# A decode step of gated attention plus a gated feed-forward on one core: the rows of Wd split unevenly over the partitions, and 31 weight rows multiplied 512 columns at a time

## The chip, the cores and the metric

One Trainium2 chip, one core of it. The metric is device time in microseconds (us) of one launch. Three runs of the kernel before gave 196.21, 196.41 and 196.93 us, a median of 196.41 us. The profile shown below is of one further execution.

## The reference

```
x = A_x                                          # 4 x 1 x 512, bf16
g = sigmoid((x * gate_w).sum(-1))
# a: attention over the last 4096 of 16384 cached positions
q = (x @ wq)                                     # 32 heads of 128; wq 512 x 4096
k, v = k_cache[:, :, -4096:], v_cache[:, :, -4096:]   # 4 batches, 8 kv heads, each used by 4 q heads
p = softmax(q k^T * 128 ** -0.5)
a = (p v) @ wo                                   # wo 4096 x 512
# b: gated feed-forward
gate, up = x @ W_gate, x @ W_up                  # 512 x 1792 each
h = gate * (gate > 0) * up
b = h @ W_down                                   # 1792 x 512
out = g * a + (1 - g) * b                        # 4 x 1 x 512
```

All inputs are bf16. The data is about 81 MB, nearly all of it the windows of the two caches, and every byte is used once for four query rows.

## The kernel before

**Stages.** The 32 pairs of batch and kv head are worked in NSET = 8 sets of four. For each set the K window (4 MB) is loaded to Ksb, transposed on TensorE by `kt` (16 fills of a PSUM bank, copied back by ACT L371 and DVE L373), multiplied with q in `scores` (L387), reduced to a maximum, exponentiated (L424), transposed on DVE (L431) and multiplied with V in `values` (L442). `combine` (L456 to L466) sums the partial results of a set and writes its scaled columns into `oq`. Ksb and Vsb hold two sets each, so the load of set s waits for the last use of set s-2.

**The end.** After the last K set, `gateup` (L468) multiplies x with W_gate and W_up and DVE makes `hT` (L477 to L487). Then TensorE runs `values` of set 7, `combine(7)`, and `product` (L542): the sum over Wd rows and wo rows that makes the output. Wd here is 1792 rows laid out as 14 rows on each of 128 partitions (`Vsb`, slot 0). wo is 32 rows on each of 128 partitions (`Wbig`). One row i is one product of a 128 x 4 stationary operand with a 128 x 512 moving operand. `product` does it as four matmuls of 128 columns, `cb` = 0 to 3, each to its own 32-partition group of bank AB, so that the four groups of the array work at once. At the end DVE and ACT copy the four quarters to `outr` (L561, L563), two engines for each half u, and SP stores it (L587).

**Queues.** All large loads are issued by SP, in this order at the end: W_gate, W_up, V of set 7, Wd (waits for `values` of set 6, ("PV", 6, 3)), then wo in pieces by WO_CUTS: rows 0 to 16, 16 to 26, 26 to 30, and rows 30 to 32 as two loads of 256 columns each ("WOL", 0 and 1). Each load has a semaphore of its own that counts to 16, one for each of the 16 DMA engines that carry it. The wo loads wait for nothing but ("Q",), far earlier; they queue behind what was issued ahead of them.

**Order on the engines.** Every engine runs its own list in the order in which `P.op` was called. PE's list near the end is: `combine(6)`, `gateup`, `values(7)`, `combine(7)`, 14 rows of Wd, then the wo rows, each group behind the wait for its load. DVE's list near the end is the four operations of `gateup`, the copy L448, three operations of `combine(7)` (L461 to L464), and the final copies.

Of the kernel before, what the change touches and what calls it, by code (L numbers as in the profile page):

```python
# [5 lines left out]
FP32 = mybir.dt.float32  # L6
BF16 = mybir.dt.bfloat16
ACTF = mybir.ActivationFunctionType
ALU = mybir.AluOpType
# [8 lines left out]
WIN = 4096  # L18
FF = 1792
NSET = 8  # L20
NFT = FF // 128
FQ = FF // 4
SCALE = DH ** -0.5
NEG = -1.0e9
LOWEST = -3.0e38
# [1 line left out]
NTR = 4  # L27
NSC = 2
NPIECE = 2
NBANK = 4  # L30
NFILL = 16
WO_CUTS = (0, 16, 26, 30)
ACT_TAKES = (0, 1, 4, 6, 8, 9, 11, 13, 14)
LOOP_FIRST = 2
LOOP_TURNS = 3
# [107 lines left out]
def bass_gated_mix__sliding_block_cached__glu_gated_reglu__decode_kernel(  # L143
# [13 lines left out]
    with ExitStack() as ctx:  # L157
        def sb(name, shape, dt):
            return ctx.enter_context(nc.sbuf_tensor(name, shape, dt))

        Ksb = sb("Ksb", [128, 2, 16384], BF16)
        Vsb = sb("Vsb", [128, 2, 16384], BF16)
# [12 lines left out]
        S32 = sb("S32", [128, 32], FP32)  # L175
        xsb = sb("xsb", [5, 512], BF16)
        xT = sb("xT", [128, 4, 32], BF16)
# [14 lines left out]
        ssum = sb("ssum", [128, 2], FP32)  # L192
        recip = sb("recip", [128, 2], FP32)
        oq = sb("oq", [128, 128], BF16)
        hrelu = sb("hrelu", [128, FQ], FP32)
        hrow = sb("hrow", [128, FQ], FP32)
        hcol = sb("hcol", [128, FQ], FP32)
        hT = sb("hT", [128, NFT * 4], BF16)
        outr = sb("outr", [4, 512], BF16)
        banks = [ctx.enter_context(nc.psum_tensor("bank%d" % i, [128, 512], FP32)) for i in range(8)]  # L200
        TR = banks[0:NTR]
        SCB = banks[NTR:NTR + NSC]
# [5 lines left out]
        Wu = Ksb[:, 0, 4 * FF:8 * FF].rearrange("p (t f) -> p t f", t=4)  # L208
        Wd = Vsb[:, 0, 0:NFT * 512].rearrange("p (i w) -> p i w", w=512)
        Wq3 = Wbig[:, :].rearrange("p (t w) -> p t w", t=4)  # L210
        Wo3 = Wbig[:, :].rearrange("p (i w) -> p i w", w=512)

        P = Program()
# [14 lines left out]
        def load_v(s):  # L228
            P.dma("sp", lambda e: e.dma_start(Vsb[:, s % 2, :], heads(A_v_cache, s)), ("V", s),
                  [("PV", s - 2, 3)] if s >= 2 else [], sem=loop_sem("V", s))  # L230
# [4 lines left out]
        for s in range(1, NSET):  # L235
# [4 lines left out]
        P.dma("sp", lambda e: e.dma_start(Ksb[:, 0, 4 * FF:8 * FF], B_W_up.rearrange("(p t) f -> p (t f)", p=128)),  # L240
              ("WU",), [("SC", NSET - 2, NBANK - 1)])
        load_v(NSET - 1)
        P.dma("sp", lambda e: e.dma_start(Vsb[:, 0, 0:NFT * 512], B_W_down.rearrange("(p i) w -> p (i w)", p=128)),
              ("WD",), [("PV", NSET - 2, 3)])
        wo_src = A_wo.rearrange("(p i) w -> p (i w)", p=128)
        for k in range(len(WO_CUTS) - 1):
            lo, hi = 512 * WO_CUTS[k], 512 * WO_CUTS[k + 1]
            P.dma("sp", lambda e, lo=lo, hi=hi: e.dma_start(Wbig[:, lo:hi], wo_src[:, lo:hi]), ("WO", k), [("Q",)])  # L248
        wo_src3 = A_wo.rearrange("(p i) w -> p i w", p=128)
        for u in range(2):  # L250
            P.dma("sp", lambda e, u=u: e.dma_start(Wo3[:, WO_CUTS[-1]:32, 256 * u:256 * u + 256],
                                                   wo_src3[:, WO_CUTS[-1]:32, 256 * u:256 * u + 256]), ("WOL", u), [("Q",)])


        P.op("pool", lambda e: e.memset(ones[:, :], 1.0), ("ONES",))
# [6 lines left out]
        for a in range(4):  # L262
            r = slice(32 * a, 32 * a + 32)
# [20 lines left out]
        P.op("dve", lambda e: e.memset(xw[:, :], 0.0), ("XW0",))  # L284
        P.op("dve", lambda e: e.memset(xT[:, :, :].rearrange("p t r -> p (t r)"), 0.0))
        P.op("dve", lambda e: e.memset(mcol[:, :], 0.0))
        P.op("dve", lambda e: e.memset(mrow2[:, :], 0.0), ("M0",))
        P.op("dve", lambda e: e.memset(qW[:, :, :, :].rearrange("p s h w -> p (s h w)"), 0.0), ("QZ",))

# [14 lines left out]
        for t in range(4):  # L304
            P.op("pe", lambda e, t=t: e.matmul(FB[:, 32:36], gwB[:, t * 128:(t + 1) * 128], xT[:, t, 0:4],
                                               start=(t == 0), stop=(t == 3)),
# [5 lines left out]
        for half in range(2):  # L312
            for t in range(4):
                for g in range(4):
# [3 lines left out]
                        start=(t == 0), stop=(t == 3), tile_position=(0, 32 * g)),  # L318
                        ("Q",) if (half == 1 and t == 3 and g == 3) else ("QH",) if (half == 0 and t == 3 and g == 3) else None,
                        [("WQ",), ("XTC",)])  # L320
        for half in range(2):
            src = SCB[half][:, :].rearrange("p (h w o) -> p h o w", h=4, o=2)
            for cc in range(2):
                dst = qrow[:, half, :].rearrange("p (h o c w) -> p h o c w", h=4, o=2, c=2)[:, :, :, cc, :]
                which = [("Q",) if half else ("QH",)]
# [6 lines left out]
        for half in range(2):  # L332
            for hh in range(4):
                for o in range(2):
                    base = 32 * half + 16 * o + hh
                    lo = 256 * hh + 128 * o
# [17 lines left out]
        def copy_done(f):  # L354
            return ("KTC",) + fills[f]
# [110 lines left out]
                 ("OQ", s), [("RECIP", s), ("G",)], sem="vd")  # L466

        def gateup():  # L468
            for which, W, key in ((0, Wg, "WG"), (1, Wu, "WU")):
                for t in range(4):  # L470
                    for g in range(4):
                        P.op("pe", lambda e, which=which, W=W, t=t, g=g: e.matmul(
                            TR[which][32 * g:32 * g + 32, 0:FQ], xT[:, t, :], W[:, t, FQ * g:FQ * g + FQ],
                            start=(t == 0), stop=(t == 3), tile_position=(0, 32 * g)),
                            ("GU", which) if (t == 3 and g == 3) else None,
                            [(key,)] + [copy_done(f) for f in range(NSET * NFILL - NTR, NSET * NFILL)])
            P.op("dve", lambda e: e.tensor_scalar(hrelu[:, :], TR[0][:, 0:FQ], 0.0, None, op0=ALU.max),  # L477
                 ("H0",), [("GU", 0)])
            P.op("dve", lambda e: e.tensor_tensor(
                hrow[:, :].rearrange("p (i c) -> p c i", i=NFT), TR[1][:, 0:FQ].rearrange("p (c i) -> p c i", i=NFT),  # L480
                hrelu[:, :].rearrange("p (c i) -> p c i", i=NFT), ALU.mult), ("H1",), [("H0",), ("GU", 1)])
            P.op("dve", lambda e: e.transpose(hcol[:, :], hrow[:, :]), ("H2",), [("H1",)])
            P.op("dve", lambda e: e.tensor_tensor(
                hT[:, :].rearrange("p (i b) -> p i b", b=4),
                hcol[:, :].rearrange("p (i b) -> p i b", b=32)[:, :, 0:4],
                gsb[:, 4:8].rearrange("p (o b) -> p o b", o=1).to_broadcast([128, NFT, 4]), ALU.mult),
                ("H",), [("H2",), ("G",)], sem="vd")  # L487
# [43 lines left out]
        for k in range(NPIECE):  # L531
            exponent(NSET - 1, k)
            turn(NSET - 1, k)
        combine(NSET - 2)
        gateup()
        for k in range(4):
            values(NSET - 1, k)
        combine(NSET - 1)
        AB = SCB[0]
        oq3 = oq[:, :].rearrange("p (b i) -> p b i", b=4)  # L540

        def product(stat, mov, cb, start, stop, name, waits):  # L542
            P.op("pe", lambda e: e.matmul(AB[32 * cb:32 * cb + 4, 0:128], stat, mov[:, 128 * cb:128 * cb + 128],  # L543
                                          start=start, stop=stop, tile_position=(0, 32 * cb)), name, waits)

        for i in range(NFT):
            for cb in range(4):
                product(hT[:, 4 * i:4 * i + 4], Wd[:, i, :], cb, i == 0, False, None,
                        [("WD",), ("H",), ("SCC", NSET - 1, NBANK - 1)])
        for k in range(len(WO_CUTS) - 1):  # L550
            for i in range(WO_CUTS[k], WO_CUTS[k + 1]):
                for cb in range(4):
                    product(oq3[:, :, i], Wo3[:, i, :], cb, False, False, None, [("WO", k), ("OQ", NSET - 1)])
        for u in range(2):
            for i in range(WO_CUTS[-1], 32):
                for cb in (2 * u, 2 * u + 1):
                    product(oq3[:, :, i], Wo3[:, i, :], cb, False, i == 31,
                            ("ACC", u) if (i == 31 and cb == 2 * u + 1) else None, [("WOL", u)])
        for u in range(2):
            for cb, eng in ((2 * u, "dve"), (2 * u + 1, "act")):  # L560
                fn = (lambda e, cb=cb: e.tensor_copy(outr[:, 128 * cb:128 * cb + 128], AB[32 * cb:32 * cb + 4, 0:128])) \  # L561
# [71 lines left out]
```

## Time and profile before

| what | value |
|---|---|
| runs | 196.21, 196.41, 196.93 us |
| the profiled execution | 196.08 us |
| its span | 194.8 us |
| HBM read | 81.01 MB, 416 GB/s over the span |
| PE busy | 135.3 us (69%) |
| DVE busy | 105.2 us (54%) |
| ACT busy | 63.8 us (33%) |
| Wd load, from issue to landing | 16.9 us |
| mean granted TensorE clock | 0.86 |

The page cuts the span into 40 slices of 4.87 us. A digit is the busy share of an engine in that slice in tenths; 9 means 90% or more. DMA is the mean busy share of the core's 16 DMA engines and GB/s what they moved. PEclk is the TensorE clock that was granted, in tenths of full speed. The chain of waits follows the last instruction back to what released it, step by step. In tables by stretch, the columns are the stretch and its length, then for each engine busy us and number of instructions, then the granted clock, the DMA share and GB/s.

The profiled execution's own time is 1.28 us over its span; what lies around the span is not seen in the trace.

### The profile page before, as it was taken

Reading aid. Unit: us, or ns where it says so; the run is one execution under the profiler, and the core shown is the slowest. Engines: PE = TensorE matmul, PEld = TensorE weight load, DVE = VectorE, ACT = ScalarE, POOL = GpSimd, SP = SyncE. Lnnn points to the kernel's source line nnn. Section 1 sums busy time; section 2 is a strip of 40 time slices with the busy share of each in tenths; the row PEclk is TensorE's granted clock in tenths of the full one; section 3 lists DMA queues with packets and bytes.
Section 4 is the critical chain, followed back from the end, with each engine's and each line's share of the span. In section 5 each row is a group of like instructions: output and inputs, shape, how many; then the busy total and the mean of one; then the engine's idle time right before and its main releaser. Section 6 shows DMA issues by size and latency. Waiting matters only on the chain.

```text
span 194.8 us, 3947 instructions
## 1 busy us (share of the span) xinstructions
PE 135.3 (69%) x1696; PEld 103.3 (53%) x1696; DVE 105.2 (54%) x282; ACT 63.8 (33%) x112; POOL 7.3 (4%) x37
## 2 busy tenths in 40 slices
PE   0135399779299929991999199929993999723834
PEld 0112387556197618860885097619762886402623
DVE  1104056896548654955594548554866595690201
ACT  2002135673055307430752065306530742310001
POOL 7300000000000000000000000000000000000000
PEclk9999669999759997999699759985999699785885
DMA  6999999999999999999999999999999999999993
GB/s 223 437 431 431 431 444 427 437 426 447 437 431 441 424 434 431 432 427 424 431 431 431 431 431 426 431 431 431 431 437 431 431 406 433 446 437 402 416 409 103
DMA packets 3885, 81.17 MB, mean 417 GB/s; under 512 B 409, under 2 KB 930, under 8 KB 1058
## 3 DMA queue, kind: packets, MB, share of 16 engines
q1 hardware_dynamic: 3864, 81.01, 97.3%
q8 instruction: 8, 0.13, 0.3%
q14 instruction: 3, 0.02, 0.0%
q10 hardware_dynamic: 10, 0.01, 0.0%
HBM read 81.01 MB, written 0.00 MB: 416 GB/s over the span
## 4 chain that ended last, share of the span: by engine, by line
DMA 60%; PE 32%; DVE 6%; issue 1%; ACT 1%; SPq 1%; DVEq 0%
DMA Ksb<-in_A_k_cache_dram 47%; PE bank L366 21%; DMA Wbig<-in_A_wo_dram 12%; PE bank L387 5%; DVE Ksb L373 3%; PE bank L442 2%; PE bank L456 2%; PE bank L543 1%; DVE sc L395 1%; DVE pT L431 1%; ACT Ksb L371 1%; DVE mq L402 0%; DVE negmax L416 0%; SPq L248 0%; SPq L581 0%
## 5 line engine op out<-in xcount | busy, mean ns | idle before, releaser
L366 PE MATMUL bank<-identw,Ksb 128*128 128x128 f32 x512 | 78.7, 316 | 26.8 <-DMA Ksb<-in_A_k_cache_dram 26.8
L366 PEld LDWEIGHTS bank<-identw,Ksb 128*128 128x128 f32 x512 | 69.5, 165 | 36.4 <-DMA Ksb<-in_A_k_cache_dram 28.6
L371 ACT COPY Ksb<-bank 128x512 f32<-128x512 f32 x72 | 41.1, 586 | 87.4 <-PE bank L366 87.3
L373 DVE COPY Ksb<-bank 128x512 f32<-128x512 f32 x56 | 37.6, 685 | 43.5 <-PE bank L366 43.4
L395 DVE CUSTOM_DVE_ANT_0 sc<-bank,mask 128x512 bf16<-128x512 f32 x32 | 21.7, 679 | 7.5 <-PE bank L387 7.3
L442 PE MATMUL bank<-Vsb,pT 128*32 128x256 bf16 x512 | 20.5, 287 | 6.9 <-DMA Vsb<-in_A_v_cache_dram 6.9
L387 PE MATMUL bank<-Ksb,qS 128*32 128x512 bf16 x256 | 20.1, 389 | 4.6 <-DVE Ksb L373 4.1
L431 DVE STREAM_TRANSPOSE pT<-sc 128x1024 bf16<-128x1024 bf16 x16 | 19.7, 1236 | 1.4 <-ACT sc L424 1.3
L442 PEld LDWEIGHTS bank<-Vsb,pT 128*32 128x32 bf16 x512 | 13.1, 100 | 13.4 <-issue 9.7
L424 ACT ACTIVATE sc<-sc,negmax 128x1024 bf16<-128x1024 bf16 x16 | 18.4, 1150 | 5.3 <-DVE negmax L416 5.2
L456 PEld LDWEIGHTS bank<-osb,Wsel 128*64 128x64 f32 x128 | 8.5, 144 | 5.3 <-issue 2.8
L456 PE MATMUL bank<-osb,Wsel 128*64 128x32 f32 x128 | 9.4, 229 | 2.0 <-DVE osb L448 2.0
L387 PEld LDWEIGHTS bank<-Ksb,qS 128*32 128x32 bf16 x256 | 4.2, 94 | 11.8 <-DVE Ksb L373 6.7
L563 ACT CAST outr<-bank 4x128 bf16<-4x128 f32 x2 | 0.5, 258 | 21.9 <-PE bank L543 21.8
L448 DVE COPY osb<-bank 128x256 f32<-128x256 f32 x8 | 3.4, 420 | 6.6 <-PE bank L442 6.6
L543 PE MATMUL bank<-Wbig,oq 128*4 128x128 bf16 x128 | 3.8, 286 | 4.2 <-DMA Wbig<-in_A_wo_dram 4.2
L298 PE MATMUL bank<-identw,xw 5*128 5x5 f32 x4 | 0.6, 263 | 8.6 <-DVE xw L292 8.6
L348 POOL COPY qS<-qW 128x64 bf16<-128x64 bf16 x8 | 1.8, 237 | 118.7 <-PE bank L387 106.4
L543 PEld LDWEIGHTS bank<-Wbig,oq 128*4 128x4 bf16 x128 | 2.8, 109 | 5.2 <-DMA Wbig<-in_A_wo_dram 5.2
L316 PE MATMUL bank<-Wbig,xT 128*32 128x512 bf16 x32 | 3.6, 631 | 2.6 <-DMA Wbig<-in_A_wq_dram 2.6
L561 DVE CAST outr<-bank 4x128 bf16<-4x128 f32 x2 | 0.6, 282 | 8.6 <-PE bank L543 8.6
L416 DVE TENSOR_SCALAR negmax<-mall 32x1 f32<-32x1 f32 x32 | 4.6, 144 | 1.0
(58 smaller groups left out, 51.2 us busy)
## 6 DMA issues: line engine op xcount, KB each, us to landing
Ksb<-in_A_k_cache_dram SPq DMA_DIRECT2D x8, 4096.0 KB, 23.4
Vsb<-in_A_v_cache_dram SPq DMA_DIRECT2D x8, 4096.0 KB, 32.5
Wbig<-in_A_wq_dram SPq DMA_DIRECT2D x1, 4096.0 KB, 12.1
Wbig<-in_A_wo_dram SPq DMA_DIRECT2D x1, 2048.0 KB, 21.4
Ksb<-in_B_W_gate_dram SPq DMA_DIRECT2D x1, 1792.0 KB, 17.5
Ksb<-in_B_W_up_dram SPq DMA_DIRECT2D x1, 1792.0 KB, 21.4
Vsb<-in_B_W_down_dram SPq DMA_DIRECT2D x1, 1792.0 KB, 16.9
Wbig<-in_A_wo_dram SPq DMA_DIRECT2D x1, 1280.0 KB, 24.0
```

What stands on the lines that cost most here:

```text
L316: P.op("pe", lambda e, half=half, t=t, g=g, col=col: e.matmul(SCB[half][32 * g:32 * g + 32, 0:512], xT[:, t, :], Wq3[:, t, col:col + 512], ...
L366: P.op("pe", lambda e, bk=bk, cc=cc, c=c, s=s: e.transpose(bk[:, cc * 128:(cc + 1) * 128], Kw[:, s % 2, c * 128:(c + 1) * 128], identw[:, :]),
L371: P.op("act", lambda e: e.copy(dst, bk[:, :]), ("KTC", s, i), [("KT", s, i)], sem="va")
L373: P.op("dve", lambda e: e.tensor_copy(dst, bk[:, :]), ("KTC", s, i), [("KT", s, i)], sem="vd")
L387: P.op("pe", lambda e, a=a, o=o: e.matmul(bk[32 * a:32 * a + 32, 0:512], qS[:, s % 2, o, :], k4[:, 16 * bank:16 * bank + 16, 32 * a:32 * a ...
L395: P.op("dve", lambda e: e.tensor_tensor_reduce(sc[:, s % 2, bank * 512:(bank + 1) * 512], bk[:, :], mask[:, :], 1.0, LOWEST, ALU.add, ALU.max,
L416: P.op("dve", lambda e, a=a: e.tensor_scalar(negmax[32 * a:32 * a + 32, par:par + 1], mall[:, 0:1], -SCALE, None, op0=ALU.mult), ("NEGMAX" ...
L424: P.op("act", lambda e: e.activation(sc[:, par, k * PW:(k + 1) * PW], sc[:, par, k * PW:(k + 1) * PW], ACTF.Exp, bias=negmax[:, par:par + ...
L431: P.op("dve", lambda e: e.transpose(pT[:, par, k * PW:(k + 1) * PW], sc[:, par, k * PW:(k + 1) * PW]), ("PTT", s, k), [("EXP", s, k), ("PV ...
L442: P.op("pe", lambda e, c=c, g=g, blk=blk: e.matmul(OB[32 * g:32 * g + 32, 0:256], pT[:, par, 32 * blk:32 * blk + 32], Vsb[:, par, 256 * bl ...
L456: P.op("pe", lambda e, k=k, lo=lo: e.matmul(FB[r, 384:416], Wsel[:, lo:lo + 64], osb[:, par, 32 * k:32 * k + 32], start=(k == 0), stop=(k ...
L543: P.op("pe", lambda e: e.matmul(AB[32 * cb:32 * cb + 4, 0:128], stat, mov[:, 128 * cb:128 * cb + 128], start=start, stop=stop, tile_positi ...
```

## The change

Three things are changed.

Wd's layout: 1792 rows are no longer 14 on each partition. The first 1408 are 11 on each of 128 partitions (NFA), and the other 384 are 6 more on each of partitions 0 to 63 (NFB). The 384 rows are brought by eight loads of eight partitions each (32q+k, 32q+k+4, ..., 32q+k+28), 6 KB a partition. `gateup` follows the layout: columns of W_gate and W_up that belong to the 384 rows go to two further PSUM banks, and DVE works the two parts one after the other; `hrow` has a part that is set to zero at the start.

The products: 11 + 6 Wd rows and the first 14 wo rows (NBULK) are each one matmul of 512 columns; row n goes to partition group n % 4 of bank DB. DB is zeroed by DVE first. When all 31 are done, DVE copies DB to `bulk`, and four fp32 matmuls with a 0/1 matrix (S32) add the four groups into AB. The other 18 wo rows go on as before.

The wo loads: WO_CUTS is (0, 14, 24, 30) in place of (0, 16, 26, 30), and rows 30 to 32 come in one load.

```diff
-NFT = FF // 128
-FQ = FF // 4
+NFA = 11
+NFB = 6
+NFT = NFA + NFB
+FQ = 32 * NFA
+FB0 = 128 * NFA
+FE = 32 * NFB
-WO_CUTS = (0, 16, 26, 30)
+WO_CUTS = (0, 14, 24, 30)
+NBULK = 14
...
-        P.dma("sp", lambda e: e.dma_start(Vsb[:, 0, 0:NFT * 512], B_W_down.rearrange("(p i) w -> p (i w)", p=128)),
+        P.dma("sp", lambda e: e.dma_start(Vsb[:, 0, 0:NFA * 512],
+                                          B_W_down[0:FB0, :].rearrange("(p i) w -> p (i w)", p=128)),
               ("WD",), [("PV", NSET - 2, 3)])
+        wd_src = B_W_down[FB0:FF, :].rearrange("(q h k i) w -> q k h (i w)", q=2, h=8, i=NFB)
+        for q in range(2):
+            for k in range(4):
+                P.dma("sp", lambda e, q=q, k=k: e.dma_start(
+                    Vsb[32 * q + k:32 * q + 32:4, 0, NFA * 512:NFT * 512], wd_src[q, k]),
+                    ("WE", q, k), [("PV", NSET - 2, 3)])
...
-        for u in range(2):
-            P.dma("sp", lambda e, u=u: e.dma_start(Wo3[:, WO_CUTS[-1]:32, 256 * u:256 * u + 256],
-                                                   wo_src3[:, WO_CUTS[-1]:32, 256 * u:256 * u + 256]), ("WOL", u), [("Q",)])
+        P.dma("sp", lambda e: e.dma_start(Wo3[:, WO_CUTS[-1]:32, :], wo_src3[:, WO_CUTS[-1]:32, :]), ("WOL",), [("Q",)])
...
+        P.op("dve", lambda e: e.memset(hrow[64:128, 32 * NFA:32 * NFT], 0.0), ("HZ",))
...
+                for t in range(4):
+                    for g in range(2):
+                        P.op("pe", lambda e, which=which, W=W, t=t, g=g: e.matmul(
+                            TR[2 + which][32 * g:32 * g + 32, 0:FE], xT[:, t, :], W[:, t, FB0 + FE * g:FB0 + FE * g + FE],
+                            start=(t == 0), stop=(t == 3), tile_position=(0, 32 * g)),
+                            ("GU", which) if (t == 3 and g == 1) else None, [(key,)] + last)
...
-        for i in range(NFT):
-            for cb in range(4):
-                product(hT[:, 4 * i:4 * i + 4], Wd[:, i, :], cb, i == 0, False, None,
-                        [("WD",), ("H",), ("SCC", NSET - 1, NBANK - 1)])
-        for k in range(len(WO_CUTS) - 1):
+        DB = SCB[1]
+        P.op("dve", lambda e: e.memset(DB[:, :], 0.0), ("DB0",), [("SCC", NSET - 1, NBANK - 1)], sem="vd")
+        rows = [(hT[:, 4 * i:4 * i + 4], Wd[:, i, :], [("WD",), ("H",)]) for i in range(NFA)]
+        rows += [(hT[0:64, 4 * i:4 * i + 4], Wd[0:64, i, :], [("WE", q, k) for q in range(2) for k in range(4)]) for i in range(NFA, NFT)]
+        rows += [(oq3[:, :, i], Wo3[:, i, :], [("WO", 0), ("OQ", NSET - 1)]) for i in range(NBULK)]
+        for n, (stat, mov, waits) in enumerate(rows):
+            g = n % 4
+            P.op("pe", lambda e, g=g, n=n, stat=stat, mov=mov: e.matmul(
+                DB[32 * g:32 * g + 4, 0:512], stat, mov, start=(n < 4), stop=(n >= len(rows) - 4),
+                tile_position=(0, 32 * g)), ("BULK",) if n == len(rows) - 1 else None, waits + [("DB0",)])
+        P.op("dve", lambda e: e.tensor_copy(bulk[:, :], DB[:, :]), ("BULKC",), [("BULK",)], sem="vd")
+        for cb in range(4):
+            product(S32[:, 0:4], bulk, cb, True, False, None, [("BULKC",), ("SCC", NSET - 1, NBANK - 2), ("WSUM",)])
+        for k in range(1, len(WO_CUTS) - 1):
             for i in range(WO_CUTS[k], WO_CUTS[k + 1]):
...
-                            ("ACC", u) if (i == 31 and cb == 2 * u + 1) else None, [("WOL", u)])
+                            ("ACC", u) if (i == 31 and cb == 2 * u + 1) else None, [("WOL",)])
```

More of the change, by code (lines that the diff above doesn't have):

```diff
@@ L194, in bass_gated_mix__sliding_block_cached__glu_gated_reglu__decode_kernel @@
         oq = sb("oq", [128, 128], BF16)
-        hrelu = sb("hrelu", [128, FQ], FP32)
-        hrow = sb("hrow", [128, FQ], FP32)
-        hcol = sb("hcol", [128, FQ], FP32)
+        hrelu = sb("hrelu", [128, 32 * NFT], FP32)
+        hrow = sb("hrow", [128, 32 * NFT], FP32)
+        hcol = sb("hcol", [128, 32 * NFT], FP32)
         hT = sb("hT", [128, NFT * 4], BF16)
         outr = sb("outr", [4, 512], BF16)
+        bulk = sb("bulk", [128, 512], FP32)
         banks = [ctx.enter_context(nc.psum_tensor("bank%d" % i, [128, 512], FP32)) for i in range(8)]
@@ L468, in gateup @@
         def gateup():
+            last = [copy_done(f) for f in range(NSET * NFILL - NTR, NSET * NFILL)]
             for which, W, key in ((0, Wg, "WG"), (1, Wu, "WU")):
@@ L474, in gateup @@
                             start=(t == 0), stop=(t == 3), tile_position=(0, 32 * g)),
[L475 to L481, printed above, removed]
+                            None,
+                            [(key,)] + last)
+                for t in range(4):
[4 more added lines that the diff above has]
+                            ("GU", which) if (t == 3 and g == 1) else None, [(key,)] + last)
+            parts = ((slice(0, 128), 0, 0, NFA), (slice(0, 64), 2, NFA, NFT))
+            for k, (r, bk, lo, hi) in enumerate(parts):
+                P.op("dve", lambda e, r=r, bk=bk, lo=lo, hi=hi: e.tensor_scalar(
+                    hrelu[r, 32 * lo:32 * hi], TR[bk][r, 0:32 * (hi - lo)], 0.0, None, op0=ALU.max),
+                    ("H0", k), [("GU", 0)])
+            for k, (r, bk, lo, hi) in enumerate(parts):
+                P.op("dve", lambda e, r=r, bk=bk, lo=lo, hi=hi: e.tensor_tensor(
+                    hrow[r, 32 * lo:32 * hi].rearrange("p (i c) -> p c i", c=32),
+                    TR[bk + 1][r, 0:32 * (hi - lo)].rearrange("p (c i) -> p c i", c=32),
+                    hrelu[r, 32 * lo:32 * hi].rearrange("p (c i) -> p c i", c=32), ALU.mult),
+                    ("H1",) if k else None, [("H0", k), ("GU", 1), ("HZ",)])
             P.op("dve", lambda e: e.transpose(hcol[:, :], hrow[:, :]), ("H2",), [("H1",)])
```

## The prediction

> **What bounds the kernel now.** I read the page's slices first.
>
> ```profile
> DMA  6999999999999999999999999999999999999993
> GB/s 223 437 431 431 431 444 427 437 426 447 437 431 441 424 434 431 432 427 424 431 431 431 431 431 426 431 431 431 431 437 431 431 406 433 446 437 402 416 409 103
> ...
> q8 instruction: 8, 0.13, 0.3%
> q14 instruction: 3, 0.02, 0.0%
> ```
>
> The DMA engines are full from the second slice to the last but one, at about 431 GB/s, 26.9 GB/s for each of 16. Nothing but the order, the amount and the spread of bytes moves the time, except in the last slice. There the chain of waits shows what ends last:
>
> ```profile
> 165.91 0.33 SPq L243
> ...
> 166.28 0.43 SPq L248
> ...
> 166.75 24.00 DMA Wbig<-in_A_wo_dram
> ...
> 190.80 1.24 PE bank L543 x30
> ...
> 192.05 0.83 PE bank L543 x20
> ...
> 192.90 0.28 DVE outr L561
> ```
>
> wo's second piece lands at 190.75; from there PE has work to 193.14, then copies and the store. Two things end close together, PE's last 64 matmuls and the last loads, as the timeline shows:
>
> ```profile
> 190.80 2.34 PE L543 MATMUL bank<-Wbig,oq 128*4 128x128 bf16 x64 [1.60 <-DMA Wbig<-in_A_wo_dram]
> 192.05 0.52 PEld L543 LDWEIGHTS bank<-Wbig,oq 128*4 128x4 bf16 x20 [0.30 <-DMA Wbig<-in_A_wo_dram]
> 192.75 0.10 PEld L543 LDWEIGHTS bank<-Wbig,oq 128*4 128x4 bf16 x4 [0.18 <-DMA Wbig<-in_A_wo_dram]
> ```
>
> The last load is in at about 192.71, and 0.43 us later PE is done. The stretches show how the loads run out:
>
> ```profile
> 188.00:190.00 2.00, 1.20 (x56) 0.91 (x44) 0.00 (x0) 0.00 (x0) 0.00 (x0) 0.54 0.98 387
> 190.00:191.00 1.00, 0.20 (x12) 0.20 (x16) 0.00 (x0) 0.00 (x0) 0.00 (x0) 0.50 0.75 274
> 191.00:191.90 0.90, 0.90 (x40) 0.75 (x30) 0.00 (x0) 0.00 (x0) 0.00 (x0) 0.50 0.53 179
> 191.90:192.40 0.50, 0.49 (x24) 0.31 (x16) 0.00 (x0) 0.00 (x0) 0.00 (x0) 0.50 0.30 88
> ```
>
> The share does not fall at once: for 0.9 us it stands at 0.53, half of the engines. The trace's semaphore increments, sixteen a load, say the same: for the last load seven arrive at 190.78 to 191.15, one at 191.64, eight at 192.48 to 192.71. **Eight engines are 1.6 us late.** The first K load's sixteen lay within 0.5 us (22.12 to 22.61), so the lag was gathered on the way. From load to load single increments jump back, after the packets of q8 and q14. The page prices them: 0.3% of 16 engines x 194.8 us is 9.4 us for 8 q8 packets, 1.2 us each; with the data packet behind it each costs its engine 1.5 us. Followed by phase, the seven q8 packets ahead of the end strike seven different engines; of the three q14 packets two strike one further engine (about 1.0 us each, so 2.0 us late and the last of all), one strikes the engine that is at 191.64.
>
> **Part 1, Wd's spread.** Each engine carries the rows of eight partitions. If the engines of partitions 0 to 63 are eight and the others eight, 14 KB x 8 = 112 KB of Wd each become 17 KB x 8 = 136 KB on one half and 88 KB on the other: 24 KB at 26.9 GB/s is 0.91 us more on the one and 0.91 us less on the other. By the packets (14336 bytes 0.54 us, 10240 bytes 0.385, 4096 bytes 0.159) the sums are 8 x 0.54 = 4.3 before, 8 x 0.42 + 8 x 0.24 = 5.3 after: 1.0 us. I take +1.0 and -0.9. Whether that helps hangs on which engines are late. The trace names none, so both bounds stay: all late ones in the half relieved, or some not.
>
> What speaks for a clean split: the count of eight; and the engines that took the small loads of x and gate_w (partitions 0 to 4) at the start, so far as they can be followed, stay early. What speaks against it: q8 strikes seven engines and q14 two that are none of these. If q8's eight packets have one half of the engines to themselves, as no engine is struck twice, then the engine that q14 struck twice lies in the other half, the one that gets 24 KB more. I hold this the likelier.
>
> [...]
>
> Their issues: SP takes 0.43 us each (L248), 8 x 0.43 = 3.5 us, so wo's first issue goes from 166.28 to about 169.8. It lands at 187.65, 18 us behind; V of set 7 and Wd are still queued, and nothing starves. Nothing else but the store waits on SP. Cover gone, it would cost 3.5 us.
>
> **Part 2, the gate and up products.** 16 more matmuls on PE and 4 more DVE operations (L477 to L482 took 2.2 us; with two parts about 3). PE then waits 6.9 us for V of set 7, DVE 6.56 us. Nothing, and up to 1 us if V came early, which it doesn't.
>
> **Part 3, 512 columns.** A 512-column matmul took 3.60 us / 32 = 0.113 at full clock (L316) or 0.55 / 8 = 0.069 (L387); at half clock I double the latter, 0.14. DB's memset stands behind `combine(7)` on DVE (ends 184.32) and writes 128x512: 0.6 as L477. So Wd's 17 rows start at 184.95, not 183.50, and end by 186.9 at the latest. wo's first piece is now two rows smaller: 256 KB / 431 = 0.6 us earlier. On the late engines that is 187.65 - 0.6 + 1.0 = 188.1. Then 14 x 0.14 = 2.0, the copy to `bulk` 0.69 (L373), four fp32 matmuls (L366: 32 in 6.17, 0.77 for four) and handovers 0.2: 191.7 at worst, 190.8 if clock or overlap help. wo's second piece lands at 190.76 - 0.6 + 1.0 = 191.2. At worst 0.5 us of delay, but the third piece comes only at 192.01 + 1.05 = 193.06, after 40 matmuls (1.24): 192.9. The cover holds, just. Zeroing `hrow` is at the start, behind the 21 us K load.
>
> **Part 4, the end.** wo's second piece loses no rows (10), the third grows from 4 to 6: 24 matmuls at 0.031 = 0.75. One last load in place of two: 512-byte rows took 0.38 for 8 KB an engine where 26.9 GB/s gives 0.30, so 2 KB rows save up to 0.1 us. But eight matmuls, not four, follow the last landing: +0.13.
>
> **The sum,** with the twice-struck engine in the loaded half: third piece 193.06, + 0.75 = 193.8; last load 192.71 + 1.0 = 193.7; eight matmuls 0.25 and the pipeline's end 0.2: 194.2 to 194.3 against 193.14. That is +1.1, from 196.08 of the profiled execution to 197.2; the median is 0.33 above that execution, so **197.5 us**, own range 197.2 to 197.9.
>
> **Rivals.**
> *A, clean split: faster.* All eight late engines lie in the relieved half. They end at 192.71 - 0.9 = 191.8, the others at 191.15 + 1.0 = 192.1. Third piece 191.4 + 0.75 = 192.15, then 0.45: PE ends at 192.6, -0.5. 195.9 us. For it: eight of sixteen. Against: the q14 engine. If TensorE were at full clock here (0.50 in all four stretches above) another 0.15.
> *B, mixed: no change.* Late ones relieved, but the engine at 191.64 is in the loaded half: 192.6, and PE 193.2, +0.05. 196.5. So too if loads of eight rows spread over all 16 engines and the change doesn't shift anything: 196.5.
> *C, the small loads cost: slower still.* If each of eight loads costs its engines what the second of the last two cost over its bytes, 0.08 us, 8 x 0.08 = 0.64 on top of the forecast: 198.1. It decides where the loaded half ends last. The gap between the loads' increments would show it; against it, such loads queue back to back in this trace.
>
> [...]
>
> **Chances.** Forecast 0.58, A 0.22, B 0.13, C 0.07. 0.5% is 0.98 us, about what a measurement of this kernel can tell from no change. The forecast's +1.1 lies just beyond: three quarters of it are slower, 0.43, with C 0.50. A reaches -0.65 and hardly beyond: faster 0.06. Same is the rest, 0.44. The range takes in A at 195.8 and the forecast's top, 197.9; C and a larger gain are left out.
>
> **What would show it.** The increments of the last load: seven or eight at about 192, one or more at 193.5 to 193.7 (forecast); all by 192.1 (A); one at 192.6 (B). In the stretches the DMA share falls to one or two sixteenths for a microsecond or more (forecast), or from 0.9 to 0 within 0.4 us (A). The `bulk` copy has to end before wo's second piece lands; if PE's last matmuls wait for it, part 3 was wrong. If q8 or q14 strike other engines, or at other times, the forecast is wrong for that reason.

## The result and the profile after

| | before | changed |
|---|---|---|
| median of the runs | 196.38 us (4 runs) | 197.62 us (4 runs, 197.50 to 198.00) |
| ratio | | 1.0061, 95% interval 1.0037 to 1.0086 |
| the same on another occasion | 196.44 us | 197.48 us; 1.0046, interval 1.0030 to 1.0062 |
| profiled execution, its span | 196.08, 194.8 us | 197.50, 196.3 us |
| last increment of the last load | 192.71 | 193.84 |
| from there to the issue of the store | 0.82 us | 1.11 us |

The changed kernel is slower by 1.0 to 1.2 us. Both intervals lie above 1; whether the loss is more than the 0.5% that the prediction took as the least to be told from no change stays open, since both reach below it. Its page has the same full slices, and what ends last is again the load of wo:

```profile
DMA  6999999999999999999999999999999999999990
GB/s 215 434 461 447 434 434 431 441 422 427 437 427 417 434 424 421 436 424 427 427 427 427 434 441 429 441 434 434 427 441 441 427 383 455 445 392 420 423 373 23
...
q8 instruction: 7, 0.11, 0.2%
q14 instruction: 3, 0.02, 0.0%
```

The chain of waits (start, us, what) of the changed kernel:

```profile
166.33 0.77 SPq L255
...
172.83 20.38 DMA Wbig<-in_A_wo_dram
...
193.26 1.04 PE bank L568 x32
...
194.32 0.28 DVE outr L595
```

SP issues the eight small loads of Wd from 166.33 to 171.83. wo's third piece is issued after them and lands 20 us later, at 193.21: the issue is not late, the queue is long. Only 32 matmuls are left behind it. Before, a piece of wo that landed at 190.75 left 64. The end has moved from a PE that was as late as the loads to the loads alone. The stretches (columns as before: stretch, length, busy us and count for PE, PEld, DVE, ACT, POOL, then clock, DMA share, GB/s) show the loads of the changed kernel running out:

```profile
190.00:191.00 1.00, 0.21 (x5) 0.02 (x5) 0.69 (x1) 0.00 (x0) 0.00 (x0) 0.50 0.76 305
191.00:192.00 1.00, 1.00 (x32) 0.70 (x36) 0.00 (x0) 0.00 (x0) 0.00 (x0) 0.50 0.42 156
192.00:193.00 1.00, 0.66 (x27) 0.37 (x16) 0.00 (x0) 0.00 (x0) 0.00 (x0) 0.50 0.12 47
193.00:194.00 1.00, 0.74 (x32) 0.64 (x32) 0.00 (x0) 0.00 (x0) 0.00 (x0) 0.50 0.03 10
```

Before, half of the engines worked to 192 and all were done at 192.71. Now thirteen are done by 192.0, and for almost two microseconds a share of 0.12 and then 0.03 is left: two engines of sixteen, then half of one on average. This is the tail that was forecast. The increments, read from the trace's semaphore records, name them. A load of eight rows has nine entries, eight of its own and one at its issue (167.48 for the first small load); that this one stands for the other eight of the 16 that the kernel waits for is the author's reading:

```
first small Wd load, changed kernel: 180.16 180.25 180.26 180.30 180.37 | 180.86 | 182.08 182.32
last load, changed kernel: 189.97 190.06 190.15 | 191.36 ... 191.99 (ten) | 192.40 | 193.58 193.84
last load, before:         190.77 ... 191.14 (seven) | 191.64 | 192.48 ... 192.71 (eight)
```

Of the eight engines that were given more, five were early, one half a microsecond behind and two about 2 us behind. The last landing is these two. So rivals A and B fall: A had no late engine among those that got more, B only the one in the middle.

### The profile page after: what moved, and what is told of

It is laid out like the page before. It is cut to its first block, busy times and chain, and to the rows that moved or that the text cites. A ratio compares the mean times of both kernels' runs of the same rounds, so it can differ in the third digit from the quotient of the medians.

```text
span 196.3 us, 3849 instructions
## 1 busy us (share of the span) xinstructions
PE 137.9 (70%) x1639; PEld 103.0 (52%) x1639; DVE 106.8 (54%) x287; ACT 63.8 (32%) x112; POOL 7.3 (4%) x37
## 4 chain that ended last, share of the span: by engine, by line
DMA 57%; PE 31%; DVE 5%; SPq 3%; issue 1%; ACT 0%; DVEq 0%
DMA Ksb<-in_A_k_cache_dram 47%; PE bank L378 21%; DMA Wbig<-in_A_wo_dram 10%; PE bank L399 5%; DVE Ksb L385 3%; SPq L255 3%; PE bank L454 2%; PE bank L468 2%; DVE sc L407 1%; DVE pT L443 1%; PE bank L568 1%; SPq L261 0%; ACT Ksb L383 0%; DVE mq L414 0%; DVE negmax L428 0%
## 5 line engine op out<-in xcount | busy, mean ns | idle before, releaser
L378 PE MATMUL bank<-identw,Ksb 128*128 128x128 f32 x512 | 78.6, 316 | 26.9 <-DMA Ksb<-in_A_k_cache_dram 26.9
L468 PE MATMUL bank<-osb,Wsel 128*64 128x32 f32 x128 | 8.9, 224 | 1.9 <-DVE osb L460 1.9
L310 PEld LDWEIGHTS bank<-identw,xw 5*128 5x128 f32 x4 | 0.5, 207 | 8.5 <-DVE xw L304 8.5
L414 DVE TENSOR_REDUCE mq<-mx 32x1 f32<-32x4 f32 x32 | 4.6, 143 | 0.8
L339 DVE CAST qrow<-bank 128x512 bf16<-128x512 f32 x2 | 1.3, 686 | 5.2 <-PE bank L328 5.2
```

The lines of the kernel that those rows point to most:

```text
L378: P.op("pe", lambda e, bk=bk, cc=cc, c=c, s=s: e.transpose(bk[:, cc * 128:(cc + 1) * 128], Kw[:, s % 2, c * 128:(c + 1) * 128], identw[:, :]),
L414: P.op("dve", lambda e, a=a: e.tensor_reduce(mq[:, a:a + 1], mx[32 * a:32 * a + 32, par, :], AXIS.X, ALU.max), ("MAXQ", s, a), [("SCC", s, ...
L468: P.op("pe", lambda e, k=k, lo=lo: e.matmul(FB[r, 384:416], Wsel[:, lo:lo + 64], osb[:, par, 32 * k:32 * k + 32], start=(k == 0), stop=(k ...
```

## The experiments

Each is the changed kernel or the kernel before with some part of the change taken out or put in, or with a small addition. Ratios are to the kernel before, run alongside on the same chip. The diffs show the lines that matter; `...` stands for the rest.

**The spread alone.** The kernel before with the uneven Wd; every product in 128 columns, wo cut as before.

```diff
-WO_CUTS = (0, 14, 24, 30)      # to the changed kernel
+WO_CUTS = (0, 16, 26, 30)
-        DB = SCB[1]
...
+        for i in range(NFT):
+            n = 128 if i < NFA else 64
+            for cb in range(4):
+                product(hT[0:n, 4 * i:4 * i + 4], Wd[0:n, i, :], cb, i == 0, False, None, ...)
```

> The kernel before with the uneven spread of Wd alone: 128-column products throughout (17 rows of Wd are 68 of them), wo cut as before, two last loads. Theory 1: the last landing moves by +0.9 us and nothing else does: 196.4 + 0.9 = 197.3 us, ratio 1.0046. Theory 2 (the products are what costs): 196.4 us, ratio 1.000. Theory 3 (the eight small loads cost by themselves, SP's 5.5 us of issue or 0.08 us a load): 197.9 us or more.

Measured: 197.32 us, ratio 1.0031 (1.0017 to 1.0045), so 0.3 to 0.9 us; the expected 1.0046 lies just outside. Theories 2 and 3 fall by this. The profiled execution had its last increment at 194.29. Its small loads show four early engines, one in the middle and three behind (the first: 180.11 to 180.50, 180.90, 181.96, 182.08, 182.72), so here one more of the loaded engines is late than in the changed kernel; the very last is 2.0 to 2.6 us behind the early ones in both. Its latest engine was already 0.6 us later than in the kernel before when V of set 7 landed (179.09 against 178.45), so its last increment overstates the step. On one engine the increments of the eight small loads stand 0.22 to 0.26 us apart, 0.235 on average, in all traces of this layout; 6 KB at 26.9 GB/s take 0.23. They cost their bytes and nothing beside.

**Wd even, the rest of the change kept.**

```diff
-NFA = 11
-NFB = 6
+NFA = 14
+NFB = 0
...
```

> The change with Wd spread evenly again (14 rows on each partition, one load); the 512-column products and the single last load stay. Theory 1 (the uneven spread adds 0.9 us to the engines that are already late, the single last load adds 0.28 us, the products add nothing): the last increment of the last load falls from 193.85 to about 192.8, the time is about 196.4 + 0.28 = 196.7 us, ratio 1.0015 to the kernel before, and about 0.9 us under the changed kernel. Theory 2 (the products and their copy through DVE hold up the end): the time stays near 197.6 us, ratio 1.006.

Measured: 196.60 us, ratio 0.9993 (0.9980 to 1.0006). The loss is gone, which is theory 1, and theory 2 (the products hold up the end) falls. But 1.0015 was expected, for the single last load, and the times do not show it (the spans do, in part; see the end of this section). The trace does: its last increment is at 192.87, 0.16 us after that of the kernel before, and the store is issued 1.10 us behind it:

```profile
192.28 1.03 PE L555 MATMUL bank<-Wbig,oq 128*4 128x128 bf16 x32 [0.60 <-DMA Wbig<-in_A_wo_dram]
193.34 0.54 ACT L583 CAST outr<-bank 4x128 bf16<-4x128 f32 x2 [21.52 <-PE bank L555]
193.34 0.60 DVE L581 CAST outr<-bank 4x128 bf16<-4x128 f32 x2 [3.40 <-PE bank L555]
193.97 0.35 SPq L607 DMA_DIRECT2D out_dram<-outr  x1
```

**The single last load alone.** The kernel before with one load for rows 30 and 31.

```diff
-        for u in range(2):
-            P.dma("sp", lambda e, u=u: e.dma_start(Wo3[:, WO_CUTS[-1]:32, 256 * u:256 * u + 256], ...
+        P.dma("sp", lambda e: e.dma_start(Wo3[:, WO_CUTS[-1]:32, :], wo_src3[:, WO_CUTS[-1]:32, :]), ("WOL",), [("Q",)])
...
```

> The kernel before with rows 30 and 31 of wo in one load, and nothing else. Theory 1 (with a single last load both pairs of final copies wait for the last landing): from the last increment to the issue of the store 1.1 us in place of 0.82; the last landing itself 0.06 to 0.1 us earlier; the time is 0.2 us over the kernel before, ratio 1.001. Theory 2 (the copies are hidden either way): ratio 0.9995 or less.

Measured: 196.72 us, ratio 1.0014 (1.0000 to 1.0029). As expected, at the edge of what can be told. One point was not: the last landing was to come 0.06 to 0.1 us earlier, and this trace has it 0.24 us later than the first one. Counted from the landing of V of set 7 it came 0.12 us earlier (14.14 us behind it, against 14.26). Its timeline:

```profile
191.14 2.25 PE L541 MATMUL bank<-Wbig,oq 128*4 128x128 bf16 x64 [1.21 <-DMA Wbig<-in_A_wo_dram]
193.42 0.54 ACT L561 CAST outr<-bank 4x128 bf16<-4x128 f32 x2 [22.17 <-PE bank L541]
193.42 0.59 DVE L559 CAST outr<-bank 4x128 bf16<-4x128 f32 x2 [7.51 <-PE bank L541]
194.04 0.35 SPq L585 DMA_DIRECT2D out_dram<-outr  x1
```

The last increment is at 192.95. Both copies of each engine begin at 193.42, behind it; the store is issued at 194.04, 1.09 us after the increment. Before, the first pair began at 192.90, 0.19 us after the last increment, as the first half's load had come earlier; the store was issued 0.82 us after it.

**The products alone.** Wd even, two last loads, the 512-column products and the new cuts kept.

> Wd even and the last rows in two loads as in the kernel before, the 512-column products alone kept. Theory 1: from the last increment to the store 0.68 us (as in the run with two last loads) in place of 0.82, since 36 fewer matmuls stand at the end of PE's list; the landing as in the kernel before; 0.1 us faster than it, ratio 0.9993, and 0.2 us faster than the run with Wd even and one last load. Rival (the copy of DB through DVE costs): ratio 1.002 or more.

Measured: 196.46 us, ratio 1.0001 (0.9991 to 1.0011). The products neither cost nor gain. The trace has the expected 0.68 us from the last increment (193.14) to the store:

```profile
192.47 0.99 PE L557 MATMUL bank<-Wbig,oq 128*4 128x128 bf16 x32 [0.88 <-DMA Wbig<-in_A_wo_dram]
193.16 0.60 ACT L585 CAST outr<-bank 4x128 bf16<-4x128 f32 x2 [20.97 <-PE bank L557]
193.17 0.62 DVE L583 CAST outr<-bank 4x128 bf16<-4x128 f32 x2 [2.59 <-PE bank L557]
193.82 0.35 SPq L609 DMA_DIRECT2D out_dram<-outr  x1
```

The 0.14 us that this wins behind the last landing is less than runs differ.

**Two last loads in the changed kernel.** The same edit the other way.

> The changed kernel with rows 30 and 31 of wo in two loads of 256 columns as before. Theory 1: the first pair of final copies starts ahead of the last landing again, so that one copy (0.28 us) leaves the end; 512-byte packets give back up to 0.1 us. The time is 0.2 to 0.28 us under the changed kernel: about 197.4 us, ratio 1.005. Theory 2 (the last landing alone sets the end, the copies are hidden either way): no gain, or 0.1 us slower.

Measured: 197.54 us, ratio 1.0044 (1.0029 to 1.0059). The ratio is as expected. The gain over the changed kernel is not seen: beside 1.0061 it would be there, beside the second measurement, 1.0046, not. The trace has 0.68 us from the last increment to the store in place of 1.11, but its last increment is at 194.24.

**The changed kernel again,** on the chip of the single last load alone and of the products alone.

> The changed kernel itself, beside the next two on one chip: 197.6 us, ratio 1.006 to the kernel before. Theory 1 (lags by instruction fetches): the eight small loads show five early engines, one in the middle and two behind once more.

Measured: 197.48 us, ratio 1.0046 (1.0030 to 1.0062), and the pattern of the small loads once more (180.29 to 180.63, 180.90, 181.79, 182.71). The three parts alone (0.0031 for the spread, 0.0014 for the single last load, 0.0001 for the products) also make 0.0046, but two pairs speak against so exact a sum: products and single last load together gave 0.9993, spread and products together 1.0044.

**The further rows on the other partitions.** Wd's six further rows on partitions 64 to 127.

```diff
-                    Vsb[32 * q + k:32 * q + 32:4, 0, NFA * 512:NFT * 512], wd_src[q, k]),
+                    Vsb[64 + 32 * q + k:64 + 32 * q + 32:4, 0, NFA * 512:NFT * 512], wd_src[q, k]),
... (and `gateup` and the products of these rows, moved to partitions 64 to 127)
```

> The changed kernel with the six further rows on partitions 64 to 127 in place of 0 to 63, in loads of eight rows as before. Theory 1a (a load of eight rows runs on the same eight engines wherever its partitions are): the increments of the eight small loads look as in the changed kernel, five together, one 0.5 us and two 1.8 to 2.1 us later, and the time is the same, 197.6 us. Theory 1b (the engine follows the partition): the loads run on the other eight, three early and five late or so; the latest of these was some 0.1 to 0.2 us ahead of the very last, so the time is 197.3 to 197.6 us, but the pattern of the increments is another.

Measured: 200.94 us, ratio 1.0208 (1.0183 to 1.0234), which neither theory gave. The increments of the first small load are 180.49 to 180.82 (five), 181.76, 183.41 and 184.34: five, one and two, as 1a has it, so the loads run on the same eight engines. But from load to load an engine's increments stand 0.4 to 0.6 us apart in place of 0.235, and the slices and stretches show what that does:

```profile
GB/s 224 466 460 427 420 420 417 427 427 458 447 427 424 427 417 422 433 424 447 440 420 433 433 433 422 427 427 447 440 420 433 406 422 465 424 391 238 336 371 20
```

```profile
180.00:182.00 2.00, 2.00 (x44) 1.55 (x36) 0.00 (x0) 0.00 (x0) 0.00 (x0) 0.50 1.05 222
182.00:184.00 2.00, 1.42 (x26) 1.12 (x18) 0.44 (x2) 0.00 (x0) 0.00 (x0) 1.00 1.15 260
184.00:186.00 2.00, 0.56 (x8) 0.27 (x11) 1.12 (x4) 0.00 (x0) 0.00 (x0) 0.85 0.95 215
```

For six microseconds all sixteen engines are busy (share 0.95 to 1.15) and move about half of their rate, 215 to 260 GB/s (the changed kernel moves 417 to 434 in the same three stretches, at a share of 0.99 to 1.04). Both groups of eight are slowed, not only the one with the small loads: in the packet records a 6 KB packet takes 0.46 us in place of 0.23, and a 14 KB packet of wo's first piece 0.99 to 1.07 us in place of 0.54. Why is not shown: no run tells which partitions the engines without small loads write in that time.

**Which engine is late.** The kernel before with eleven tiny loads behind Wd's.

```diff
+        for r in PROBES:                       # 1, 2, 3, 4, 5, 6, 7, 8, 10, 12, 14
+            P.dma("sp", lambda e, r=r: e.dma_start(probe[0:r, 256 * r:256 * r + 256], A_wq[0:r, 0:256]), ("PROBE", r), [("Q",)])
...
```

> The kernel before with eleven tiny loads (1, 2, 3, 4, 5, 6, 7, 8, 10, 12 and 14 rows of 512 bytes) put in SP's queue behind Wd's load; the first of the final copies waits for them too, so that they are done at the end. They carry nothing that is used. If a load of r rows runs on r of the sixteen engines, always the same first r, the increments of the loads nest: each longer load shows those of the shorter one and one more, and so the lag of each engine by its number is read. Theory 1: of the first eight, five are early, one is 0.5 us and two are 1.5 to 2.0 us behind; of engines 8 to 15 most are behind. Rival (the lag belongs to loads, not to engines): the increments of one load lie together or do not nest. Time: up to 0.5 us over the kernel before, since engine 0 takes eleven more packets.

Measured: 197.41 us, one run, beside 196.30. The increments nest:

```
1 row:  181.06
2 rows: 181.24 182.04
3 rows: 181.11 181.43 182.22
4 rows: 181.29 181.61 182.40 183.31
5 rows: 181.24 181.48 181.79 182.60 183.49
6 rows: 181.43 181.66 182.00 182.76 182.78 183.68
7 rows: 181.05 181.62 181.84 182.20 182.96 182.96 183.87
8 rows: 181.25 181.34 181.82 182.01 182.38 183.13 183.17 184.05
```

Each line is the one above, some 0.19 us later, with one more. Numbering the engines in the order in which the loads call them in, engine 0 is early, 1 is 1.0 us behind it (0.6 behind the last of the early ones), 2 early, 3 is 2.2 us behind, 4 early, 5 is 1.7 us behind, 6 and 7 early. In the longer loads 8 and 9 are early, one of 10 and 11 is early and one late, 12 and 13 are late. The sixteen increments of Wd's load itself (nine early, one in the middle, six late) leave one early and one late for 14 and 15. The expected 0.5 us at most was too little. Engine 3, the last, carries eight of these loads. From Wd's last increment to that of wo's first piece it is 5.61 us (183.11 to 188.72) in place of 4.89 in the first trace, so a load of 512 bytes a row cost it 0.09 us. That is less than the 0.19 us between the increments, but several times its bytes at 26.9 GB/s (0.02).

**More fetches for DVE.** The changed kernel with 110 one-element memsets at the head of DVE's list.

```diff
+        for f in range(110):
+            P.op("dve", lambda e, f=f: e.memset(filler[0:1, f:f + 1], 0.0))
...
```

> The changed kernel with 110 one-element memsets more at the head of DVE's list, which only move DVE's instructions on by nearly one fetch of 8 KB. Theory 1 (an engine is late because instruction fetches struck it; the q14 packets are DVE's and go to two engines in turn): there are four q14 packets in the span in place of three, the earlier ones come some 35 us sooner, and the engine in the middle (0.5 us behind) is struck twice: of the eight that carry the small Wd loads five are early and three 1.5 to 2.1 us behind, none in the middle. The time stays within 0.3 us of the changed kernel, since the latest engine is the same. Rival (the lags are the engines' own): five, one and two as before.

Measured: 198.41 us, one run, beside 196.30. There are four q14 packets, at 6.4, 54.5, 79.0 and 130.8. After the first, one engine is late by about 1.0 us in the first K load already (fifteen increments at 22.20 to 22.68, one at 23.45). At the end the small loads show five early, one 0.8 us, one 2.0 and one 3.2 us behind. So here a fetch made an engine late, and these are DVE's. Two points of the expectation were wrong: the engine in the middle was not struck again, but the latest one was (three strikes, 3.2 us), so the packets do not go to two engines simply in turn; and therefore the time rose, by about the 1.0 us that one strike costs.

**The same runs by their spans.** A launch's time is 1.2 to 2.7 us over its span, and this part differs from launch to launch within one kernel. The span of every run is on record to 0.1 us. The table gives the mean span less that of the kernel before, run alongside, with an interval of about 95% from the scatter of the runs:

| run | what it has of the change | span, us over the kernel before |
|---|---|---|
| the spread alone | spread | 0.91 (0.81 to 1.01) |
| the products alone | products | 0.08 (-0.01 to 0.17) |
| the single last load alone | last load | 0.18 (0.07 to 0.29) |
| Wd even | products, last load | 0.16 (0.08 to 0.24) |
| two last loads | spread, products | 1.16 (1.01 to 1.31) |
| the changed kernel again | all three | 1.11 (0.95 to 1.27) |

The spread is nearly the whole loss, and the single last load adds some 0.1 to 0.2 us to an even kernel. Beside the spread it adds nothing that shows.

## Why the prediction was right

*The bound.* Right. The end is set by the engines that finish the loads last, and these are late by instruction fetches. The run with more of DVE's fetches shows this as cause; it is one run. For PE's (q8) it is argued: the steps in the increments follow their packets, and the packets move with PE's list. With 16 more gate and up matmuls in that list the sixth came at 172.8 to 174.0 in all six traces with the uneven Wd, at 182.4 to 183.1 in the five with Wd even. No run took them away. So the prediction's last sign, q8 at other times, did show (172.76 in place of 182.39) and did no harm: the latest engine is the one that q14 struck twice, and q14's packets came when they had come before (43.9, 78.9 and 120.1). A q8 packet took 0.93 to 1.11 us; the 1.2 us of the prediction came from a rounded share.

*The spread.* The choice between the two bounds was right: engines that were late got 24 KB more. The step was put as "+1.0". In the two first traces the latest engine goes from V of set 7 to the end in 14.26 us before (178.45 to 192.71) and 15.15 us after (178.69 to 193.84), +0.9; the rest of the +1.13 between the last increments was there when V landed. The other traces agree: 15.10 to 15.22 us in the three further ones with the small loads on partitions 0 to 63 and nothing else added, 14.14 to 14.29 in the three with Wd even and no tiny loads. The 24 KB at 26.9 GB/s are 0.91. The spread alone gave 0.3 to 0.9 us in the times and 0.91 in the spans.

*The reason given for that choice* was half wrong. It said that q8's fetches have one half of the engines to themselves and that the engine struck twice by q14 is therefore in the other. The tiny loads show q8's on 5, on one of 10 and 11, on 12, 13 and one of 14 and 15. One of them is in the loaded half. q14's are 1 and 3, so the engine in question does lie there. So the choice came out right although half of its reason was wrong, and that is in part luck. A second late engine, 5, lies in the loaded half too: by the same working, at 192.5 and 0.9 us, it would have left no gain even without 3. Also, that the engines which took the small loads of x and gate_w stay early holds for 0 and 2, not for 1 and 3.

*The small loads.* The issue of the eight small loads of Wd was put at 0.43 us each; it was 0.62 to 0.77, 5.5 us together. It was hidden, as foreseen, by the 20 us queue. Rival C (0.64 us more) falls with the 0.235 us between increments. These loads of 48 KB in a full queue took 0.235 us an engine, 0.23 of it their bytes.

*Engines and partitions.* That the rows of partitions 0 to 63 lie on eight engines, and those of 64 to 127 on the other eight, was the author's assumption; no run shows it. What the runs showed: a tiny load of r rows (r from 1 to 8) always took the same first r engines, by the nesting of the increments; the trace does not give their numbers. The eight small loads showed five early, one in the middle and two behind on partitions 0 to 63 (the first: 180.16 to 180.37, 180.86, 182.08, 182.32) and again on 64 to 127 (180.49 to 180.82, 181.76, 183.41, 184.34). And the latest engine went from V of set 7 to the end in 15.15 us in place of 14.26.

*The 512-column products.* Right that they are hidden, and as close as said. The timeline of the changed kernel:

```profile
184.84 0.48 DVE L572 MEMSET bank<- 128x512 f32 x1
...
185.47 2.39 PE L578 MATMUL bank<-Vsb,hT 128*4 128x512 bf16 x17 [1.49 <-DVE bank L572]
...
188.32 1.87 PE L578 MATMUL bank<-Wbig,oq 128*4 128x512 bf16 x14 [0.46 <-DMA Wbig<-in_A_wo_dram]
...
190.24 0.69 DVE L581 COPY bulk<-bank 128x512 f32<-128x512 f32 x1 [4.91 <-PE bank L578]
...
191.39 1.26 PE L568 MATMUL bank<-Wbig,oq 128*4 128x128 bf16 x40
...
193.26 1.03 PE L568 MATMUL bank<-Wbig,oq 128*4 128x128 bf16 x32 [0.60 <-DMA Wbig<-in_A_wo_dram]
```

wo's first piece came at 188.28 (forecast 188.1), PE started on the second at 191.39 (second landing 191.35, forecast 191.2), and PE then waited 0.60 us for the third. The cover holds. One size was off: Wd's 17 rows were to end by 186.9 at the latest. They started at 185.47, 0.5 us late, and took 2.39 us, 0.14 each, the half-clock price that the prediction used for wo's rows (granted clock 0.56 from 185 to 188); they ended at 187.86, still 0.46 us ahead of wo. (The prediction's remark that the clock was 0.50 in all four stretches holds for three of them; the first has 0.54.)

*The end.* Mis-sized. "Eight matmuls, not four, follow the last landing: +0.13" left out the copies. With two loads the first pair of copies starts before the second half's sums are done; with one load all four wait, two in a row on each engine. From last increment to store it is 1.1 us in place of 0.82, +0.28. Every trace with a single last load has 1.09 to 1.12; with two it is 0.80 to 0.83 with the 128-column products and 0.68 with the 512-column ones. In the spans the single last load costs 0.18 us by itself and nothing that shows beside the spread, so its size in the whole stays open.

*The sum.* +1.1 forecast. The two first traces give 0.9 + 0.28, the times 1.24 and 1.04, the spans 1.11. The forecast put 1.0 on the spread, a little too much, and 0.13 on the end, where the copies were missing. The two errors have opposite signs, so that the median came within 0.12 us of the forecast is partly luck.

No version beat the kernel before. By these lags a spread by halves has nothing to gain, though no run tried the other direction: 1, 3 and 5 are behind in the one half, four or more in the other, and what the one is spared the other gets. In the first trace the eight late ones end within 0.23 us (192.48 to 192.71).

## What to carry to other kernels

When the DMA engines are the bound, look at when each of the sixteen finishes, not at their mean share: a share of a half at the end was here eight engines at work while eight had ended. Before bytes are moved from late engines to early ones, find out which number is late, with tiny loads of 1, 2, 3 ... rows, since one late engine among those that get more can take the whole gain, as engine 3 did here (+0.9 us). When the last load is merged, count what then stands behind it, the copies too: here 1.11 us in place of 0.82.

## What the runs showed of the hardware

An instruction fetch among the loads cost one engine here far more than its bytes: 8 KB of DVE's took 0.31 us in its own packet and left the engine about 1.0 us late (the run with more fetches for DVE, first K load: fifteen increments at 22.20 to 22.68, one at 23.45). The 16 KB packets of q8, taken here as PE's, about 1.0 us each, left it 1.5 us late (the second K load of the kernel before: fifteen increments at 31.82 to 32.32, one at 33.82, behind the packet at 30.66). These lags were not made up: in the kernel before, the last increment of the W_gate load came 2.02 us behind its first (162.42, 164.44), that of the last load still 1.94 us (190.77, 192.71).

While the eight small loads wrote partitions 64 to 127 beside the large loads, all sixteen engines together moved about half of their rate: 222 GB/s at a busy share of 1.05 from 180 to 182 us, where the changed kernel, with the small loads on partitions 0 to 63, moved 434 at 1.04.
